# Column-layout attention: the softmax sums of two batches inverted on 112 partitions by way of small matmuls

## The chip, the cores and the metric

One core of one Trainium2 chip. The time is that of one execution on the device, in microseconds; it is the median of several runs. Beside these runs one execution was taken by the hardware profiler, and every row below is from that one.

## The reference

Attention over 4 batches, 12 heads, 448 positions and 64 dimensions, with a root-mean-square norm on q and k, then two feed-forward layers over the 1792 tokens:

```python
q_n, k_n = (rmsnorm(q, g_q), rmsnorm(k, g_k))
scores = scale * np.matmul(q_n, k_n.transpose(0, 1, 3, 2))
scores = scores - np.max(scores, axis=-1, keepdims=True)
attn = np.exp(scores)
attn = attn / (np.sum(attn, axis=-1, keepdims=True) + 1e-09)
attn_out = np.matmul(attn, v)
x = attn_out.transpose(0, 2, 1, 3).reshape(B * S, H * D)
g = x @ w_gate
x = (g * (1.0 / (1.0 + np.exp(-g))) * (x @ w_val)) @ w_out
h = x @ w_in
return (h * np.cos(h)) @ w_out2
```

## The kernel before

The work is done on pairs of heads: 4 batches by 6 pairs, 24 pairs in all. A pair's 896 query rows are 7 tiles of 128. The first two batches, pairs 0 to 11, are done in a first stage of their own, and they alone are touched by the change. Batches 2 and 3 have another way through attention, which runs beside the matmuls of the first feed-forward layer in the second stage. The second feed-forward layer follows.

In the first stage the scores are held transposed: keys on partitions, queries along the row. The stage is a list of steps (c_step, line 735), seven for each pair, which run from the first loads to step NCB + CXX + CXL. Each step calls, in this order: c_st (one tile of transposed scores, a matmul for q times k and one that takes off the row maximum, then the exponential on ScalarE, line 702), c_av (the exponentials times v in f32, line 712, in four parts a pair, at steps 1, 3, 5 and 6 after a shift of CAV), c_x, c_lo, c_s (scores ten steps ahead, only to find the maximum on VectorE, lines 669 and 670), c_row (the maxima turned into a row by a small matmul and copied to SBUF on ScalarE, lines 676 to 682, two steps ahead of the pair) and the preparation of later pairs: squares, the norm's power on GpSimd, scaling, the split into two f16 parts (h), and a DMA transpose into T. A scale (line 347) stands ahead of the power.

c_av writes two banks a pair, t and u, one for each head. The stationary operand has v in 64 of its columns and ones in the other 64, so that a bank holds the unnormalised output of the head in one half of its partitions and, in each of the 64 partitions of the other half, the same sum of exponentials. There is one bank t and one bank u, so the next pair's first c_av waits until both have been read. c_x (line 714) reads them with four ScalarE copies of 64 partitions by 448: the sums into r (lines 719 and 721, with 1e-9 added) and the outputs into ov (lines 720 and 722, scaled). It takes the reciprocal of all of r, 128 x 448, on VectorE (line 723), multiplies (line 726) and makes the high f16 part of x (line 727). Four steps later c_lo makes the low part on GpSimd (line 733). x is read by the second stage alone.

The order of the instructions is set by a planner, which takes them in the order in which they are written as their operands come free in its own timeline. In the first stage SyncE's DMAs and GpSimd's instructions are held in the order written (the InOrder helper, line 156); on TensorE the helper keep_in_program_order pins one instruction behind the one written just before it. PSUM has three banks "s" (c_s, c_row and small sums share them), three banks "c" for c_st, and t and u. After the first stage, banks c and u become part of the four banks "mm" of the second stage. The second stage begins with a score matmul of pair 12 (line 479, which needs its T), and then visits: 18 matmuls each, over three pairs' x (lines 1053 to 1055).

Of the kernel before, what the change touches and what calls it, by code (L numbers as in the profile page):

```python
# [9 lines left out]
F32 = mybir.dt.float32  # L10
# [4 lines left out]
AF = mybir.ActivationFunctionType  # L15
ALU = mybir.AluOpType
AX = mybir.AxisListType
PSUM = bass.MemoryType.PSUM
A0 = {'raw0': 2, 'h160': 1, 'sq0': 1, 'pr0': 6, 'T0': 2}
COL = {'B': 3, 'C': 3, 'w': 3, 'r': 2, 'o': 2, 'V': 2}  # L20
A1 = {'p16': 2, 'PT': 1, 'sq': 1, 'pr': 3, 'sm': 10, 'R': 1, 'rv': 1, 'raw': 1, 'h16': 1, 'T': 2}
CF = ('kl xl ql qm kf', 'rp vh nm xl qm sa 2', 'ql xl 0 2 5 6', 'ql xl 0 3 4 6')
LA = 5
# [7 lines left out]
CXX = 8  # L31
# [3 lines left out]
VMQ = 30  # L35
VMR = 8
VMO = 10
CXL = 4
VM2 = 46
CC1 = 22  # L40
CC2 = 29
# [123 lines left out]
def kernel(ctx: ExitStack, tc, q, k, v, g_q, g_k, w_gate, w_val, w_out, w2_in, w2_out, out):  # L165
    nc = tc.nc
# [3 lines left out]
    B, H, S, D = q.shape  # L170
    P = 128
    CO = 384
    NP = H // 2
# [9 lines left out]
    HP = P // 2  # L183
# [21 lines left out]
    ps_s = ctx.enter_context(tc.tile_pool(name="ps_s", bufs=3, space=PSUM))  # L205
# [7 lines left out]
    def xy_tile(more=False):  # L213
        return xy_pools[int(more)].tile([P, 2, S], F16, tag="xy", name="xy")

    def tmp():
        return tmp_p.tile([P, S], F32, tag="tmp", name="tmp")

    def bank(pool, tag):
        return pool.tile([P, 512], F32, tag=tag, name=tag)  # L220


    ident = const.tile([P, P], F32, name="ident")
# [12 lines left out]
    vs2 = const.tile([P, 2], F32, name="vs2")  # L236
# [38 lines left out]
    pools = {}  # L275
# [12 lines left out]
    NS = 2 * S // P  # L288
    NE = (NS + 1) // 2
    NB = NP * NS  # L290
    NCB = NC * NS
    prep = {}
# [96 lines left out]
    def x_inv(b):  # L389
        return vsc[:, 2 * b + 1:2 * b + 2]  # L390
# [225 lines left out]
    def ctile(nm, shape, dt, g=None):  # L616
        return c_p.tile(shape, dt, tag="c" + nm, name="c" + nm, bufs=COL[nm])

# [17 lines left out]
    def c_v(g):  # L636
        V = colv[g % 2]
        for h in range(2):
            hs = slice(HP * h, HP * h + HP)
            src = v[g // NP, 2 * (g % NP) + h].rearrange("(q t) d -> q t d", t=NS)  # L640
            sync.dma_start(V[:HP, :4 - h, h, hs], src[:, 0:NS - h:2])
            sync.dma_start(V[HP:, :3, h, hs], src[:, 1:NS:2])
            if h:
                sync.dma_start(V[HP:, 3, h, hs], src[:, NS - 1])

    def c_T(g):
        pg = prep[g]
        T = pg["T"] = pool("T", g).tile([P, 2 * NS, P], F16, tag="T", name="T")
        sync.dma_start_transpose(T, pg["h16"].rearrange("p g d -> p (g d)"))

    def c_copy(g):
        pg = prep[g]
        T = pg["T"]
        Bq = pg["B"] = ctile("B", [P, NS, P], F16)
        C = colc[g % 3][0]
        nc.vector.tensor_copy(Bq[:HP], T[HP:, :NS])
        nc.vector.tensor_copy(T[HP:, :NS], T[:HP, :NS])
        nc.scalar.activation(C[:HP], T[:HP, NS:], AF.Copy)

    def c_s(n):  # L660
        g, t = divmod(n, NS)
        pg = prep[g]
        if t == 0:
            pg["m"] = pools["sm"].tile([P, 3, 8], F32, tag="sm", name="sm")
        ps = bank(ps_s, "s")
        T = pg["T"]
        for h in range(2):
            hs = slice(HP * h, HP * h + HP)
            nc.tensor.matmul(ps[hs, :S].rearrange("p (t q) -> p t q", q=HP), T[:, t, hs], T[:, NS:, h::2], start=True, stop=True)
        nc.vector.tensor_reduce(pg["m"][:, 0, t:t + 1], ps[:, :S], axis=AX.X, op=ALU.max)  # L670

    def c_row(g):
        pg = prep[g]
        W = colc[g % 3][1]
        m = pg["m"][:, 0, :NS]
        nc.vector.tensor_scalar(W[:, :, 0], m, 2.0 ** -14, None, op0=ALU.mult)
        nc.vector.scalar_tensor_tensor(W[:, :, 32], m, 2.0 ** -14, W[:, :, 0], op0=ALU.mult, op1=ALU.subtract)
        for t0, t1 in ((0, 4), (4, NS)):
            ps = bank(ps_s, "s")
            for t in range(t0, t1):  # L680
                nc.tensor.matmul(ps[HP:, (t - t0) * P:(t - t0 + 1) * P], W[:, t], id16, start=True, stop=True)
            nc.scalar.activation(
                pg["B"][HP:, t0:t1], ps[HP:, :(t1 - t0) * P].rearrange("p (t q) -> p t q", q=P), AF.Copy,
            )

    def c_st(n):
        g, i = divmod(n, NS)
        pg = prep[g]
        T, Bq, C = pg["T"], pg["B"], colc[g % 3][0]
        ps = bank(ps_c, "c")  # L690
        h0, j = CT[i]
        e = col[g, i] = pool("pr", g, n).tile([P, S], F32, tag="pr", name="pr")
        for k, (wt, off, mv) in enumerate(((T, NS, T), (C, 0, Bq))):
            for h in ((0, 1) if h0 is None else (h0,)):
                hs = slice(HP * h, HP * h + HP)
                rows = hs if h0 is None else slice(0, P)
                k0 = (off + 2 * j) * P + h
                w = wt.rearrange("p t q -> p (t q)")[:, k0:min(k0 + 2 * P - 1, (off + NS) * P):2]
                nc.tensor.matmul(
                    ps[rows, :S].rearrange("p (t q) -> p t q", q=HP), w, mv[:, :NS, hs], start=(k == 0), stop=(k == 1),  # L700
                )
        nc.scalar.activation(e, ps[:, :S], AF.Exp, scale=esc)

    def c_av(g, j):
        pg = prep[g]
        if j == 0:
            pg["o"] = (bank(ps_t, "t"), bank(ps_u, "u"))
        for h in range(2):
            hs = slice(HP * h, HP * h + HP)
            rows = slice(0, P) if j < 3 else hs  # L710
            e = col[g, 2 * j + h] if j < 3 else col[g, NS - 1]
            nc.tensor.matmul(pg["o"][h][:, :S], colv[g % 2][rows, j, h], e[rows], start=(j == 0), stop=(j == 3))

    def c_x(g):
        pg = prep.pop(g)
        o = pg["o"]
        r, ov = ctile("r", [P, S], F32), ctile("o", [P, S], F32)
        vb = vs2[:, g // NP:g // NP + 1]
        nc.scalar.activation(r[:HP], o[0][HP:, :S], AF.Copy, bias=1e-9)
        nc.scalar.activation(ov[:HP], o[0][:HP, :S], AF.Copy, scale=vb[:HP])  # L720
        nc.scalar.activation(r[HP:], o[1][:HP, :S], AF.Copy, bias=1e-9)
        nc.scalar.activation(ov[HP:], o[1][HP:, :S], AF.Copy, scale=vb[HP:])
        nc.vector.reciprocal(r, r)
        x = X[g] = xy_tile()
        xs = tmp()
        nc.vector.tensor_tensor(xs, ov, r, op=ALU.mult)
        nc.scalar.activation(x[:, 0], xs, AF.Copy)
        xlo[g] = xs

# [2 lines left out]
    def c_lo(g):  # L732
        gps.tensor_sub(X[g][:, 1], xlo.pop(g), X[g][:, 0])

    def c_step(n):
        if 0 <= n < NCB:
            c_st(n)
        m = n - CAV
        if m >= 0 and m % NS in (1, 3, 5, 6) and m < NCB:
            c_av(m // NS, (1, 3, 5, 6).index(m % NS))  # L740
        m = n - CXX
        if m >= 0 and m % NS == 0 and m < NCB:
            c_x(m // NS)
        m = n - CXX - CXL
        if m >= 0 and m % NS == 0 and m < NCB:
            c_lo(m // NS)
        m = n + CSM
        if 0 <= m < NCB:
            c_s(m)
        m = n + CRW  # L750
        if m >= 0 and m % NS == 0 and m < NCB:
            c_row(m // NS)
        if n < NCB:
            s_prep(n)

    PREP = (
        ("load", p_load), ("vload", p_vload), ("sqk", lambda g: p_sq(g, 1)), ("sqq", lambda g: p_sq(g, 0)),
# [6 lines left out]
    def ph(g):  # L764
        return 2 if g < NC else 2 + g // NP
# [3 lines left out]
    def s_prep(n):  # L769
        for nm, f in PREP:  # L770
            for g in range(NPAIR):
                if NS * g + OFF[ph(g)][nm] - (CSH if g < NC else 0) == n:
                    if g < NC and nm in ("vhi", "vlo"):
                        continue
                    if g < NC and nm == "vload":
                        c_v(g)
                    elif g < NC and nm == "T":
                        c_T(g)
                    elif g < NC and nm == "sw":
                        c_copy(g)  # L780
                    else:
                        f(g)
# [466 lines left out]

    for n in range(1 - LEAD, NCB + CXX + CXL + 1):  # L1250
        for f, at in ((v_max, 0), (v_row, VMR), (v_out, VMO)):
# [38 lines left out]
    for bn, per in blocks:  # L1290
# [15 lines left out]
        for qn in range(per):  # L1306
# [3 lines left out]
            kind, c = pc["kind"], pc["c"]  # L1310
# [47 lines left out]
    for c in range(NH):  # L1358
        j0 = j
        j += 2  # L1360
        for b in range(B):
            ps = [bank(ps_s, "s"), bank(ps_t, "t")] if nh % 3 == 2 else [bank(ps_m, "mm") for _ in range(2)]
# [28 lines left out]
    while j < len(pieces):  # L1391
        ps = [None] * nt
# [49 lines left out]
```

## Time and profile before

| | |
|---|---|
| median of 3 runs | 1311.82 us (1310.14 to 1314.35) |
| the profiled execution | 1312.33 us |
| its span, first to last instruction | 1310.6 us |
| TensorE busy, share of the span | 1201.9 us, 92% |
| VectorE (DVE) busy | 858.2 us, 65% |
| ScalarE (ACT) busy | 661.3 us, 50% |
| GpSimd (POOL) busy | 404.4 us, 31% |
| mean granted TensorE clock | 0.974 of full speed |

The shares are averages over stages with different limits. In the rows further down, PE is TensorE's matmuls and PEld its weight loads, L719 is line 719 of the kernel, and an arrow stands for "waits for" or "made from". An f32 matmul shows as two instructions, one for each of its passes.

### The profile page before, as it was taken

How to read it: one execution, taken by the hardware profiler on the slowest of the kernel's cores; microseconds unless marked ns; L12 is line 12 of the kernel's file. 1: busy time of each engine (PE TensorE's matmuls, PEld its weight loads, DVE VectorE, ACT ScalarE, POOL GpSimd, SP SyncE). 2: the span in 40 equal slices, each digit the busy share in tenths (PEclk: the TensorE clock that was granted, in tenths of full speed). 3: DMA queues.
4: the chain of work that ended last, by engine and by line, in shares of the span. 5: the costliest groups of instructions: out<-in, count | busy, mean ns of one | idle time of the engine just before them, and what ended most of it. 6: DMA issues, size and time to landing. Idle time of an engine off the chain costs nothing. (4 is left out here: it accounts for less than half of the span.)

```text
span 1310.6 us, 18041 instructions
## 1 busy us (share of the span) xinstructions
PE 1201.9 (92%) x6460; PEld 677.1 (52%) x6460; DVE 858.2 (65%) x1555; ACT 661.3 (50%) x1246; POOL 404.4 (31%) x309
## 2 busy tenths in 40 slices
PE   1888797989889998999999999999999998999998
PEld 0333233444665446844468555855555545666665
DVE  5888966989978897067854498477788886100000
ACT  3677565656456543265653455457777775100000
POOL 7645302433622345035453013504332322000000
PEclk9799898999989999999999999999999999999999
DMA  5534734678797879579668697640112237522121
GB/s 139 138 73 82 191 99 118 179 187 228 225 247 221 204 208 287 183 175 225 150 133 257 235 315 263 235 157 1 50 49 73 73 133 261 177 72 94 61 91 43
DMA packets 218425, 207.34 MB, mean 158 GB/s; under 512 B 143584, under 2 KB 173792, under 8 KB 218336
## 3 DMA queue, kind: packets, MB, share of 16 engines
q1 hardware_dynamic: 218336, 206.20, 55.5%
q8 instruction: 50, 0.82, 0.2%
q14 instruction: 39, 0.32, 0.1%
HBM read 134.35 MB, written 41.53 MB: 134 GB/s over the span
## 5 line engine op out<-in xcount | busy, mean ns | idle before, releaser
L1053 PE MATMUL mm<-xy,wp 128*128 128x448 f16 x840 | 297.5, 355 | 2.7 <-DVE ga L1092 2.6
L1054 PE MATMUL mm<-xy,wp 128*128 128x448 f16 x840 | 297.2, 354 | 0.0
L1055 PE MATMUL mm<-xy,wp 128*128 128x448 f16 x840 | 295.6, 354 | 0.0
L1066 PEld LDWEIGHTS <-g 128*128 128x128 f16 x1344 | 131.5, 98 | 91.0 <-issue 4.1
L1053 PEld LDWEIGHTS <-wp 128*128 128x128 f16 x960 | 95.8, 100 | 99.8 <-issue 19.2
L1055 PEld LDWEIGHTS <-wp 128*128 128x128 f16 x960 | 94.5, 98 | 87.4 <-issue 2.0
L1054 PEld LDWEIGHTS <-wp 128*128 128x128 f16 x960 | 94.7, 99 | 84.5 <-issue 5.7
L156 POOL TENSOR_TENSOR g<-tmp,g 128x448 f16<-128x448 f32 x64 | 71.0, 1122 | 175.7 <-ACT g L1212 175.7
L1053 PE MATMUL mm<-g,wp 128*128 128x448 f32 x288 | 108.3, 376 | 3.8 <-ACT mm L1113 2.6
L1054 PE MATMUL mm<-g,wp 128*128 128x448 f32 x288 | 106.8, 371 | 1.7 <-POOL g L156 1.7
L1055 PE MATMUL mm<-g,wp 128*128 128x448 f32 x288 | 106.3, 370 | 0.0
L156 POOL TENSOR_TENSOR g<-ga,g 128x448 fp32r<-128x448 f32 x48 | 68.3, 1436 | 112.2 <-ACT g L1102 111.8
L1066 PE MATMUL mm<-wp,g 128*128 128x384 f16 x576 | 99.2, 326 | 3.7 <-DVE tmp L1208 3.7
L1066 PE MATMUL s<-wp,g 128*128 128x384 f16 x576 | 99.3, 326 | 0.0
L156 POOL TENSOR_TENSOR wp<-w,wp 128x768 fp32r<-128x768 f32 x36 | 70.3, 1958 | 74.4 <-ACT wp L993 42.8
L498 ACT ACTIVATE pr<-s,sm,esc 128x448 f32<-128x448 f32 x84 | 60.2, 717 | 62.2 <-DVE sm L492 55.5
L488 DVE TENSOR_REDUCE sm<-s 128x1 f32<-128x448 f32 x84 | 51.0, 615 | 44.1 <-PE s L479 44.1
L1224 ACT ACTIVATE tmp<-mm,osc 128x384 f32<-128x384 f32 x8 | 4.6, 580 | 148.6 <-PE mm L1066 147.8
L156 POOL TENSOR_TENSOR ri<-ss,half 128x14 f32<-128x14 f32 x24 | 63.3, 2639 | 41.6 <-DVE ss L347 32.8
L893 DVE SCALAR_TENSOR_TENSOR w<-raw,w 128x768 int32<-128x768 int32 x68 | 75.1, 1107 | 0.5
L894 DVE SCALAR_TENSOR_TENSOR w<-raw,w 128x768 int32<-128x768 int32 x68 | 75.0, 1104 | 0.5
L156 POOL TENSOR_TENSOR p<-pr,p 128x448 f16<-128x448 f32 x36 | 42.4, 1181 | 100.4 <-ACT p L522 65.0
(174 smaller groups left out, 2263.2 us busy)
## 6 DMA issues: line engine op xcount, KB each, us to landing
raw<-in_moe_w_out_dram SPq DMA_DIRECT2D x28, 768.0 KB, 5.8
raw<-in_moe_w_in_dram SPq DMA_DIRECT2D x16, 768.0 KB, 5.8
raw<-in_moe_w_gate_dram SPq DMA_DIRECT2D x12, 768.0 KB, 5.8
raw<-in_moe_w_val_dram SPq DMA_DIRECT2D x12, 768.0 KB, 5.6
wp<-scr_gate SPq DMA_DIRECT2D x24, 384.0 KB, 4.5
w<-scr_out SPq DMA_DIRECT2D x24, 384.0 KB, 4.2
wp<-scr_val SPq DMA_DIRECT2D x24, 384.0 KB, 5.0
wp<-scr_out SPq DMA_DIRECT2D x24, 384.0 KB, 3.0
```

Of the source, the lines that this page charges most:

```text
L156: r = f(*args, **kw)
L488: nc.vector.tensor_reduce(sm[:, 0, t:t + 1], slot[n][:, :S], axis=AX.X, op=ALU.max)
L498: nc.scalar.activation(e, slot.pop(n)[:, :S], AF.Exp, bias=sm[:, 1, t:t + 1], scale=esc, accum_out=sm[:, 2, t:t + 1],)
L893: nc.vector.scalar_tensor_tensor(wi, hi, -0x40000000, wi, op0=ALU.bitwise_and, op1=ALU.bitwise_or)
L894: nc.vector.scalar_tensor_tensor(wi, lo, 29, wi, op0=ALU.logical_shift_right, op1=ALU.bitwise_or)
L1053: nc.tensor.matmul(ps[f][:, :S], wh[:, s], x[:, 0], start=(first and i == 0), stop=False)
L1054: nc.tensor.matmul(ps[f][:, :S], wh[:, s], x[:, 1], start=False, stop=False)
L1055: nc.tensor.matmul(ps[f][:, :S], wl[:, s], x[:, 0], start=False, stop=(last and i == n - 1))
L1066: nc.tensor.matmul(ps[:, :CO], x[:, a, p0:p0 + P], rhs, start=st, stop=sp)
L1224: nc.scalar.activation(osb, ps[:, :CO], AF.Copy, scale=ci)
```

## The change

c_x now copies the two banks whole, 128 partitions by 448, on ScalarE, and is done. One step later c_inv moves the sums: for each of four pieces of 112 queries and each head, a matmul with the copied bank as the stationary operand and one column of the identity as the moving one puts the 112 sums of that piece on 112 partitions. The eight results are eight columns of one s bank. VectorE adds 1e-9 and scales them (one instruction) and takes the reciprocal, 112 x 8. One step on, c_back brings them back: eight matmuls with such a column, repeated 64 times, as the stationary operand and the identity as the moving one, into the halves of another s bank. One step on, c_mul multiplies on VectorE, half by half and straight from the bank, and makes the high part of x. c_lo comes eight steps after c_x in place of four. The tiles r are gone, the tiles o are four in place of two.

```diff
--- before.py
+++ after.py
@@ -17,7 +17,7 @@
 AX = mybir.AxisListType
 PSUM = bass.MemoryType.PSUM
 A0 = {'raw0': 2, 'h160': 1, 'sq0': 1, 'pr0': 6, 'T0': 2}
-COL = {'B': 3, 'C': 3, 'w': 3, 'r': 2, 'o': 2, 'V': 2}
+COL = {'B': 3, 'C': 3, 'w': 3, 'o': 4, 'V': 2}
 A1 = {'p16': 2, 'PT': 1, 'sq': 1, 'pr': 3, 'sm': 10, 'R': 1, 'rv': 1, 'raw': 1, 'h16': 1, 'T': 2}
 CF = ('kl xl ql qm kf', 'rp vh nm xl qm sa 2', 'ql xl 0 2 5 6', 'ql xl 0 3 4 6')
 LA = 5
@@ -35,7 +35,11 @@
 VMQ = 30
 VMR = 8
 VMO = 10
-CXL = 4
+CXL = 8
+CXI = 1
+CXB = 2
+CXM = 3
+QC = 112
 VM2 = 46
 CC1 = 22
 CC2 = 29
@@ -712,18 +716,43 @@
             nc.tensor.matmul(pg["o"][h][:, :S], colv[g % 2][rows, j, h], e[rows], start=(j == 0), stop=(j == 3))
 
     def c_x(g):
+        pg = prep[g]
+        o = pg["o"]
+        ov = pg["ov"] = [ctile("o", [P, S], F32) for _ in range(2)]
+        for h in range(2):
+            nc.scalar.activation(ov[h], o[h][:, :S], AF.Copy)
+
+    def c_inv(g):
+        pg = prep[g]
+        ps = bank(ps_s, "s")
+        for c in range(4):
+            for h in range(2):
+                one = HP - HP * h
+                tc.keep_in_program_order(nc.tensor.matmul(
+                    ps[:QC, 2 * c + h:2 * c + h + 1], pg["ov"][h][:, QC * c:QC * c + QC], ident[:, one:one + 1], start=True, stop=True,
+                ))
+        r = pg["r"] = pools["sm"].tile([P, 3, 8], F32, tag="sm", name="sm")
+        nc.vector.tensor_scalar(r[:QC, 0], ps[:QC, :8], 1e-9, x_inv(g // NP)[:QC], op0=ALU.add, op1=ALU.mult)
+        nc.vector.reciprocal(r[:QC, 1], r[:QC, 0])
+
+    def c_back(g):
+        pg = prep[g]
+        ps = pg["rb"] = bank(ps_s, "s")
+        r = pg["r"]
+        for c in range(4):
+            for h in range(2):
+                tc.keep_in_program_order(nc.tensor.matmul(
+                    ps[HP * h:HP * h + HP, QC * c:QC * c + QC], r[:QC, 1, 2 * c + h:2 * c + h + 1].to_broadcast([QC, HP]),
+                    ident[:QC, :QC], start=True, stop=True,
+                ))
+
+    def c_mul(g):
         pg = prep.pop(g)
-        o = pg["o"]
-        r, ov = ctile("r", [P, S], F32), ctile("o", [P, S], F32)
-        vb = vs2[:, g // NP:g // NP + 1]
-        nc.scalar.activation(r[:HP], o[0][HP:, :S], AF.Copy, bias=1e-9)
-        nc.scalar.activation(ov[:HP], o[0][:HP, :S], AF.Copy, scale=vb[:HP])
-        nc.scalar.activation(r[HP:], o[1][:HP, :S], AF.Copy, bias=1e-9)
-        nc.scalar.activation(ov[HP:], o[1][HP:, :S], AF.Copy, scale=vb[HP:])
-        nc.vector.reciprocal(r, r)
         x = X[g] = xy_tile()
         xs = tmp()
-        nc.vector.tensor_tensor(xs, ov, r, op=ALU.mult)
+        for h in range(2):
+            hs = slice(HP * h, HP * h + HP)
+            nc.vector.tensor_tensor(xs[hs], pg["ov"][h][hs], pg["rb"][hs, :S], op=ALU.mult)
         nc.scalar.activation(x[:, 0], xs, AF.Copy)
         xlo[g] = xs
 
@@ -738,12 +767,10 @@
         m = n - CAV
         if m >= 0 and m % NS in (1, 3, 5, 6) and m < NCB:
             c_av(m // NS, (1, 3, 5, 6).index(m % NS))
-        m = n - CXX
-        if m >= 0 and m % NS == 0 and m < NCB:
-            c_x(m // NS)
-        m = n - CXX - CXL
-        if m >= 0 and m % NS == 0 and m < NCB:
-            c_lo(m // NS)
+        for f, d in CEND:
+            m = n - CXX - d
+            if m >= 0 and m % NS == 0 and m < NCB:
+                f(m // NS)
         m = n + CSM
         if 0 <= m < NCB:
             c_s(m)
@@ -752,6 +779,8 @@
             c_row(m // NS)
         if n < NCB:
             s_prep(n)
+
+    CEND = ((c_x, 0), (c_inv, CXI), (c_back, CXB), (c_mul, CXM), (c_lo, CXL))
 
     PREP = (
         ("load", p_load), ("vload", p_vload), ("sqk", lambda g: p_sq(g, 1)), ("sqq", lambda g: p_sq(g, 0)),
```

## Rows read from the trace of the kernel before

**Rows 1.** busy time by stretch: length, PE, PEld, DVE, ACT, POOL, clock, DMA

```profile
155.97:178.38 22.41, 16.36 (x71) 6.40 (x71) 14.24 (x28) 11.16 (x19) 2.79 (x3) 0.85 0.27 67
178.38:190.78 12.40, 11.20 (x56) 4.97 (x55) 9.77 (x20) 10.23 (x18) 1.04 (x1) 1.00 0.37 110
...
52.57:215.90 163.33, 136.61 (x575) 54.16 (x574) 137.17 (x216) 115.59 (x207) 57.86 (x43) 0.92 0.45 112
```

**Rows 2.** waits of TensorE's matmuls, 52.57 to 215.90: total, times, longest

```profile
PE s L681 <- DVE cw L677: 8.4, 3, 5.9
PE s L669 <- DVE sm L670: 4.0, 5, 1.1
PE s L669 <- ACT cB L682: 3.4, 3, 1.6
PE t L712 <- ACT pr L702: 3.2, 4, 1.2
PE c L699 <- ACT cB L682: 2.9, 2, 1.7
PE s L681 <- DVE vm L365: 2.9, 1, 2.9
PE s L681 <- DVE ss L347: 1.5, 1, 1.5
```

**Rows 3.** groups by line, 52.57 to 215.90: busy us, mean ns | idle before

```profile
L723 DVE RECIPROCAL cr<-cr 128x448 f32<-128x448 f32 x11 | 32.4, 2947 | 1.1 <-ACT cr L721 0.8
...
L720 ACT ACTIVATE co<-t,vs 64x448 f32<-64x448 f32 x11 | 6.9, 628 | 0.1
L726 DVE TENSOR_TENSOR tmp<-co,cr 128x448 f32<-128x448 f32 x11 | 6.8, 616 | 0.4 <-ACT pr L702 0.4
L719 ACT ACTIVATE cr<-t 64x448 f32<-64x448 f32 x12 | 6.5, 540 | 9.5 <-PE u L712 9.3
```

**Rows 4.** busy time by stretch, the stretch just behind, columns as in rows 1

```profile
222.00:262.00 40.00, 40.00 (x214) 19.41 (x212) 34.36 (x67) 20.99 (x41) 16.97 (x11) 0.95 0.55 146
```

**Rows 5.** single lines: count, ns min/median/max (L904: busy us, mean ns)

```profile
L1208 DVE SCALAR_TENSOR_TENSOR tmp<-tmp,mm x44: 606/621/623, 882.1 to 1098.0; 128x448 f32<-128x448 f32 x44
...
L904 DVE RECIPROCAL wsc<-winv 128x1 f32<-128x1 f32 x1 | 0.2, 164 | 0.0
...
L1113 ACT ACTIVATE mm<-mm x36: 533/541/547, 343.7 to 861.2; 128x448 f32<-128x448 f32 x36
```

**Rows 6.** timeline of TensorE from 178.68: start, length, instruction, count

```profile
178.68 0.50 PE L919 MATMUL s<-nm,full 128*128 128x1 f32 x4
...
179.04 0.54 PE L699 MATMUL c<-cB,cC 128*128 128x448 f16 x2
...
179.51 0.79 PE L669 MATMUL s<-T 128*64 128x448 f16 x6
```

**Rows 7.** timeline of TensorE, the last c_av of the third pair

```profile
95.28 0.64 PE L712 MATMUL t<-pr,cV 64*128 64x448 f32 x1
...
95.29 0.64 PE L712 MATMUL u<-pr,cV 64*128 64x448 f32 x1
...
95.76 0.54 PE L712 MATMUL t<-pr,cV 64*128 64x448 f32 x1
```

**Rows 8.** timeline, the longest wait of the row matmuls

```profile
159.14 2.93 DVE L723 RECIPROCAL cr<-cr 128x448 f32<-128x448 f32 x1
...
162.76 0.63 PE L681 MATMUL s<-id,cw 128*64 128x128 f16 x4 [5.90 <-DVE cw L677]
```

**Rows 9.** timeline, what leads to the second stage's first matmul

```profile
204.62 2.95 DVE L723 RECIPROCAL cr<-cr 128x448 f32<-128x448 f32 x1
...
207.49 0.11 DVE L347 TENSOR_SCALAR ss<-ss 128x14 f32<-128x14 f32 x1
...
220.96 0.58 PE L479 MATMUL s<-T 128*64 128x448 f16 x2 [5.09 <-DMA T<-h]
```

**Rows 10.** waits, 40 to 216, GpSimd's longest: us in total, times, longest

```profile
POOL xy L156 <- ACT xy L727: 90.3, 9, 20.9
```

## The prediction

> **What bounds the kernel now.** I read the busy times by stretch first, to see which engine leads while the changed lines run; then who made TensorE wait there; then the groups of the changed lines; then the stretch behind. The stretch is from the first L719 (52.57 us) to the twelfth (215.90): eleven intervals in 163.33 us, 14.85 each. In it DVE is busy 137.17 us, TensorE 136.61, ACT 115.59 [rows 1]. So two engines lead almost level; TensorE idles 26.7 us (163.33 - 136.61). The granted clock is 0.92 on average: 1.00 where an interval is short (12.4 us from 178.38) and 0.85 in the longest one (22.4 us from 155.97). The clock has two levels, 1.2 and 2.4 GHz, so part of each long interval ran at the lower one.
>
> The waits name the 26.7 us: 16.8 are put down to DVE (8.4 + 4.0 + 2.9 + 1.5), 9.5 to ACT (3.4 + 3.2 + 2.9) [rows 2]. The reader is to see that nobody waits for the reciprocal as such: x is not read before the next stage. It costs by standing in DVE's queue ahead of the maxima and of the row that feeds the next pair. What it costs there: 2947 ns a time, and its four ACT copies twice 540 + 628, 2.34 us (two for each of a pair's banks) [rows 3].
>
> Behind the stretch TensorE is busy 40.00 us of 40.00 [rows 4]. So I let time won or lost before it come out whole at the end, and price whatever TensorE work spills into it in full.
>
> **The change part by part.** The sums are per pair of heads; there are twelve pairs.
>
> DVE: out go the reciprocal, 2.95, and one product, 0.616 [rows 3]. In come two products of 64 rows that read PSUM; the nearest row, a product with a PSUM operand, takes 0.62, and I take that for each, since time goes with the 448 columns. In come also a scale and a reciprocal of eight columns; a reciprocal of one column takes 0.164 and I take 0.2 for each [rows 5]. That is 3.56 out, 1.64 in: 1.9 us less per pair, 23 us over twelve, none of it yet on the path.
>
> ACT: four copies of 64 rows become two of 128. A plain copy of 128 x 448 from PSUM takes 0.541 [rows 5], so 2.34 becomes 1.08: 1.26 less per pair.
>
> TensorE, first set (c_inv): eight f32 matmuls with one moving column each, and each f32 matmul stands in the trace as two passes. The nearest row has four passes of that shape, with weights of 128 columns; they start at 178.68 and the next matmul starts at 179.04, so 0.09 us a pass [rows 6]. Sixteen are 1.44 us. Below that they could be 112/128 of it, 1.26.
>
> TensorE, second set (c_back): eight f32 matmuls of 112 columns, into the upper and the lower 64 rows of a bank in turn. The nearest f32 row with two halves is the last c_av: its t and u passes run at the same time, and the second passes start 0.48 us after the first, for 448 columns [rows 7]. At 112 columns that is 0.12; in pairs 8 x 0.12 = 0.96 us, one after another 16 x 0.12 = 1.92. I take 0.96, because in the f16 row of exactly this column shape six matmuls (three pairs of 448 columns) need 0.79 us with their loads [rows 6]. Together 2.4 us a pair, between 2.2 and 3.4; twelve make 28.8. I let all of it count: c_inv is pinned behind the first c_av of the next pair and c_back behind a c_st, that is inside the run of matmuls in which TensorE itself is the bound and not in its waits.
>
> What comes off the path. (a) The four copies begin when a pair's last c_av ends, and the copy of the next pair's rows and its exponentials stand behind them on ACT. TensorE waited for ACT nine times for 9.5 us [rows 2], about 1.06 a time, against 1.26 saved: I take 8.5. (b) Of DVE's 16.8, the longest wait, 5.9 us to 162.76, has the whole reciprocal in it (159.14 to 162.07) [rows 8]: 2.9 go. Of the other 10.9 I take 6: the 2.9 behind a v maximum stay, since the change touches nothing of it, and 2 of the rest, where the maxima wait for matmuls themselves. Together 9. What is late next there is the chain of maxima itself. (c) The clock: 8% of 163.33 is 13.1 us. With 17.5 of 26.3 us of waits gone I take half, 6.5. (d) The next stage's first matmul starts at 220.96, 5.09 us late, on a transpose. That goes back to a scale at 207.49 which came out of DVE's queue right behind the reciprocal of 204.62 [rows 9]. 2.9 us go; then TensorE's own last c_av is what is late. (e) c_lo moves from four to eight steps behind c_x. On POOL, kept in program order, it waited 90.3 us for x [rows 10], and the subtractions that feed the next transposes stood behind it. Its operand now comes three steps later and it five after that, one step more of room than before; I take 1 us. No DMA is added and SP's order holds the same issues. Off together: 8.5 + 9 + 6.5 + 2.9 + 1 = 27.9.
>
> What I cost at nothing: the banks. Each set takes one of the three "s" banks, c_back's until both products are done. The cover is that DVE no longer stands for 2.95 us with three maxima behind it. Without that cover c_s waits as it does now, 4.0 us in all [rows 2]. The last pair's chain has no loss either: its x is first needed after three visits of 18 matmuls.
>
> The sum: 28.8 - 27.9 = +0.9. The profiled execution took 1312.33 us (span 1310.6, 1.7 around it); 1313.2. The median of the runs, 1311.82, is 0.5 lower, so 1312.7, given as **1313**. The pattern is an exchange: DVE is freed, and TensorE takes its place as the bound.
>
> **The rivals.** *The new matmuls fall into waits.* If the planner puts them where TensorE would still idle, the 8.8 us that I left (26.3 - 17.5) take that much of the 28.8; and with shorter gaps the clock stays up, 6.6 us more. 1312.7 - 8.8 - 6.6 = 1297. For it: TensorE at 1.00 in the interval that starts at 178.38 [rows 1], where few waits fell. Against it: the pins.
>
> *The halves don't pair (the other side).* In c_back each weight load and each pass goes alone, 1.92 instead of 0.96: 3.4 us a pair, 40.3 in all, +12.4 and 1324. The point from which it decides is 27.9 / 12 = 2.3 us of TensorE per pair; over 2.65 the whole is slower by more than a measurement can tell. For it: the 0.48 us of the f32 halves is more than twice what a pair of f16 matmuls takes in the six, 0.2. Against it: those halves do start together [rows 6, 7].
>
> The Trainium skill speaks for this rival. Its page "TensorE: Matmul & The Clock Gate", Part 3 ("The mechanism"), says that a weight load overlaps a running matmul only where its row group is another one; all of c_back's loads use the same rows, so by that rule none would be hidden. The trace doesn't hold to it for f16: the six matmuls above cover all rows and have a load each; three times 448 columns take 0.56 us at 2.4 GHz, so 0.23 is left of 0.79 for six loads and the way through the array [rows 6]. For f32 weights of half the columns no row here shows it, and this is why the rival keeps a real chance.
>
> *The copies were not the wait.* If the row copy comes late through TensorE itself, (a) and half of (b) fall away: 1312.7 + 13 = 1326. The waits speak against it, since both name ACT and DVE as last; it is in the slow cases' upper end.
>
> **How the numbers follow.** About 0.3% (3.9 us) is what a measurement of this kernel can tell from no change. The exchange has 0.42 (1305 to 1320: 0.12 faster, 0.19 same, 0.11 slower), the matmuls in the waits 0.32 (0.29 faster, 0.03 same), the halves that don't pair 0.18 and the copies that were not the wait 0.08 (0.01 same, 0.25 slower between them). Sums: faster 0.41, same 0.23, slower 0.36. The low end is the first rival with half of what c_inv may come in under its price (1 us of 2), 1296; the high end takes the last two rivals and a few us on top of 1324 for c_s waiting on banks, 1328. The likeliest case's own range is 1305 to 1320.
>
> **What would show it.** Right: in the same twelve-pair stretch DVE's busy time falls by about 21 us and TensorE's rises above DVE's by 15 or more; c_inv's sixteen passes take near 1.44 us and c_back's 0.96, with upper and lower halves starting together; TensorE's waits for DVE and ACT sum to under 12 us; the clock of the stretch is over 0.92; the last c_x starts within some 4 us of 215.90. The second stage's first matmul comes 1 to 3 us after the last c_av, not 5. Wrong: c_back's passes evenly spaced at 0.12 or more; or the waits still at 20 us; or DVE's waits now for c_back (a new term that I left out); or, on the other side, intervals all near 12 us, which would mean that the passes cost TensorE nothing.

## The result, and the profile after

| | median us | ratio to the kernel before, 95% interval |
|---|---|---|
| the kernel before, beside it | 1312.97 | |
| the changed kernel | 1321.82 (1320.42 to 1324.71, 4 runs) | 1.0085 [1.0061, 1.0109] |

The change costs 0.85%. The ratio is taken between the executions of the same chip and goes with an interval, so all comparisons below are made by ratios; times 1311.8 us it is 11.2 us (8.0 to 14.3). The profiled execution of the changed kernel took 1324.71 us, its span 1322.8. Lines of the new functions: c_x L723, c_inv L731 (matmuls), L735 and L736 (scale, reciprocal), c_back L744, c_mul L755, the high part of x L756. Lines carried over from the kernel before have numbers four higher: c_s is L673 and L674, c_row L680 to L686, c_st L703, c_av L716, and GpSimd's helper is L160.

First the busy times by stretch, the same stretch as in [rows 1], from the first c_x to the twelfth, and what follows it (columns as there).

```profile
52.44:229.40 176.96, 155.91 (x927) 79.52 (x926) 124.44 (x246) 103.40 (x187) 60.28 (x44) 0.98 0.48 114
229.40:235.32 5.92, 2.99 (x17) 2.91 (x17) 2.67 (x4) 2.69 (x6) 1.58 (x2) 0.72 0.72 141
240.00:280.00 40.00, 40.00 (x240) 20.31 (x238) 35.45 (x68) 22.48 (x46) 16.88 (x12) 1.00 0.54 148
```

The stretch is 13.6 us longer (176.96 against 163.33). TensorE is busy 19.3 us more and DVE 12.7 less, so TensorE now leads by 31. The clock went from 0.92 to 0.98. Yet TensorE is still idle for 21.05 us (176.96 - 155.91), against 26.7. The engine became the bound, and four fifths of its idle time stayed. Behind the stretch it is again busy throughout, as in [rows 4].

Next, for whom TensorE's matmuls wait there (in total, times, longest), to be held against [rows 2].

```profile
PE s L685 <- DVE cw L681: 11.1, 7, 4.5
PE s L744 <- DVE sm L736: 1.9, 1, 1.9
PE c L703 <- ACT cB L686: 1.8, 2, 1.6
PE s L673 <- ACT cB L686: 1.4, 6, 0.3
PE s L673 <- DVE tmp L755: 1.4, 1, 1.4
PE s L673 <- DVE sm L674: 1.3, 2, 1.0
PE t L716 <- ACT pr L706: 0.7, 2, 0.3
```

Waits for ACT fell from 9.5 to 3.9 us (1.8 + 1.4 + 0.7). Waits for DVE did not fall: with two more of 0.4 and 0.3 they are 16.4, against 16.8, although the 2.95 us reciprocal is gone. Together the two kinds are still 20.3 us. The waits for DVE now come seven times in eleven pairs from cw, the scaled maxima, in place of three times.

The groups of the changed lines (busy us, mean ns | idle before):

```profile
L731 PE MATMUL s<-ident,co 128*112 128x1 f32 x176 | 18.1, 233 | 0.0
L755 DVE TENSOR_TENSOR tmp<-co,s 64x448 f32<-64x448 f32 x20 | 12.4, 619 | 5.5 <-PE s L744 5.3
L744 PE MATMUL s<-ident,sm 112*64 112x112 f32 x176 | 10.6, 263 | 1.9 <-DVE sm L736 1.9
...
L681 DVE SCALAR_TENSOR_TENSOR cw<-sm,cw 128x7 f16<-128x7 f32 x10 | 6.5, 652 | 0.2
L680 DVE TENSOR_SCALAR cw<-sm 128x7 f16<-128x7 f32 x10 | 5.2, 516 | 0.2
L735 DVE TENSOR_SCALAR sm<-s,vsc 112x8 f32<-112x8 f32 x11 | 2.4, 220 | 2.6 <-PE s L731 2.6
L736 DVE RECIPROCAL sm<-sm 112x8 f32<-112x8 f32 x11 | 2.2, 196 | 0.1
```

Every single duration is near its price: copies 540 ns, products 619, scale and reciprocal 220 and 196. Two things are to be seen beside that. DVE stands idle for 5.3 us before the products, waiting for c_back. And the two little instructions that make cw take 516 and 652 ns. In the kernel before:

```profile
L677 DVE SCALAR_TENSOR_TENSOR cw<-sm,cw 128x7 f16<-128x7 f32 x10 | 4.9, 494 | 0.2
...
L676 DVE TENSOR_SCALAR cw<-sm 128x7 f16<-128x7 f32 x10 | 2.2, 218 | 0.1
```

The timeline of one interval shows how the wait comes about.

```profile
89.21 1.64 PE L731 MATMUL s<-ident,co 128*112 128x1 f32 x16
...
90.78 0.39 PE L673 MATMUL s<-T 128*64 128x448 f16 x2
...
95.10 0.99 PE L744 MATMUL s<-ident,sm 112*64 112x112 f32 x16
...
95.92 0.57 PE L673 MATMUL s<-T 128*64 128x448 f16 x4
96.14 1.25 DVE L755 TENSOR_TENSOR tmp<-co,s 64x448 f32<-64x448 f32 x2 [1.25 <-PE s L744]
...
97.42 1.16 DVE L674 TENSOR_REDUCE sm<-s 128x1 f32<-128x448 f32 x2
...
98.08 1.03 POOL L160 TENSOR_TENSOR xy<-tmp,xy 128x448 f16<-128x448 f32 x1 [7.15 <-ACT xy L756]
...
98.61 0.54 DVE L680 TENSOR_SCALAR cw<-sm 128x7 f16<-128x7 f32 x1
...
99.07 1.03 POOL L160 TENSOR_TENSOR h<-rqk,h 128x448 f16<-128x448 f32 x1
99.18 0.96 DVE L681 SCALAR_TENSOR_TENSOR cw<-sm,cw 128x7 f16<-128x7 f32 x1
...
100.20 0.58 PE L685 MATMUL s<-id,cw 128*64 128x128 f16 x7 [1.01 <-DVE cw L681]
```

c_inv needs 1.57 us until the next matmul starts, c_back 0.82. But DVE stands for 1.25 us until c_back is done, then works 1.25 us on the products, and only then come the last two maxima, cw, and the row that the next pair's scores need. The products themselves are in no hurry: x is read in the next stage.

The products do more than stand in the queue. As soon as the high part of x is made from them, GpSimd subtracts it (98.08), and in its order the split h follows (99.07). Both run beside cw, and each of cw's two instructions ends within 0.05 us of one of GpSimd's. At the 0.19 us each that they take elsewhere they would have been done 1.1 us sooner; TensorE waited 1.01 us. Four of the seven waits for cw are of this kind, 1.01 us each. The longest, 4.5 us, is another: there cw is not slow, but two instructions on the next stage's weights (w, 1.27 and 0.94 us) stand before it and between its two parts in VectorE's queue.

At the end of the stage (before: 5.57 us from the last c_x at 215.90 to the first matmul of a visit at 221.47):

```profile
229.98 0.36 PE L731 MATMUL s<-ident,co 128*112 128x1 f32 x2 [1.09 <-ACT co L723]
230.35 1.24 DVE L755 TENSOR_TENSOR tmp<-co,s 64x448 f32<-64x448 f32 x2
...
231.62 0.58 ACT L756 ACTIVATE xy<-tmp 128x448 f16<-128x448 f32 x1 [1.69 <-DVE tmp L755]
232.11 0.53 ACT L723 ACTIVATE co<-u 128x448 f32<-128x448 f32 x1
...
232.68 2.77 PE L731 MATMUL s<-ident,co 128*112 128x1 f32 x14 [2.35 <-ACT co L723]
```

It is 5.92 us now, from 229.40 to the first matmul of a visit at 235.32. The wait for the transpose is gone from there; in its place the last pair's c_inv waits twice, 3.44 us, for the copies of banks t and u. The second copy stands on ACT behind the high part of the pair before, which waits for that pair's products.

### The profile page after: what moved, and what is told of

Its sections match the earlier page's. It is cut to its first block, busy times and chain, and to the rows that moved or that the text cites. A ratio compares the mean times of both kernels' runs of the same rounds, so it can differ in the third digit from the quotient of the medians.

```text
span 1322.8 us, 18802 instructions
## 1 busy us (share of the span) xinstructions
PE 1223.4 (92%) x6844; PEld 704.8 (53%) x6844; DVE 837.1 (63%) x1579; ACT 645.7 (49%) x1222; POOL 409.2 (31%) x309
## 5 line engine op out<-in xcount | busy, mean ns | idle before, releaser
L160 POOL TENSOR_TENSOR g<-tmp,g 128x448 f16<-128x448 f32 x64 | 71.2, 1126 | 175.4 <-ACT g L1241 175.4
L160 POOL TENSOR_TENSOR g<-ga,g 128x448 fp32r<-128x448 f32 x48 | 64.4, 1353 | 121.6 <-ACT g L1131 121.4
L160 POOL TENSOR_TENSOR wp<-w,wp 128x768 fp32r<-128x768 f32 x36 | 73.6, 2050 | 78.0 <-ACT wp L1022 47.0
L160 POOL TENSOR_TENSOR p<-pr,p 128x448 f16<-128x448 f32 x36 | 44.0, 1226 | 124.0 <-ACT p L526 97.4
L922 DVE SCALAR_TENSOR_TENSOR w<-raw,w 128x768 int32<-128x768 int32 x68 | 77.5, 1145 | 0.5
L921 DVE TENSOR_SCALAR w<-raw 128x768 int32<-128x768 int32 x68 | 50.2, 744 | 37.8 <-DMA w<-scr_out 9.8
L160 POOL TENSOR_TENSOR ri<-ss,half 128x14 f32<-128x14 f32 x24 | 64.6, 2690 | 29.3 <-DVE ss L351 28.6
```

The lines of the kernel that those rows point to most:

```text
L160: r = f(*args, **kw)
L921: nc.vector.tensor_scalar(wi, hi, 3, 0x3FFFFFF8, op0=ALU.logical_shift_left, op1=ALU.bitwise_and)
L922: nc.vector.scalar_tensor_tensor(wi, hi, -0x40000000, wi, op0=ALU.bitwise_and, op1=ALU.bitwise_or)
```

## The experiments

Twelve runs, in three groups. The first takes the change's savings without its cost, the second takes parts of the cost away, the third looks for a way to have the savings without it. The runs of the first group leave out the division or give a head the wrong sums, and those with half of c_inv leave out the second head's sums: they serve for their time alone.

| run | median us | ratio, 95% interval |
|---|---|---|
| whole copies alone | 1299.09 | 0.9901 [0.9871, 0.9931] |
| no reciprocal alone | 1303.34 | 0.9924 [0.9895, 0.9954] |
| both, nothing added | 1285.53 | 0.9797 [0.9770, 0.9823] |
| changed kernel, products late | 1314.46 | 1.0025 [1.0006, 1.0045] |
| changed kernel, half of c_inv | 1314.95 | 1.0031 [1.0014, 1.0047] |
| both of these | 1308.84 | 0.9991 [0.9973, 1.0008] |
| changed kernel, no pins | 1319.12 | 1.0056 [1.0037, 1.0074] |
| aligned banks | 1343.92 | 1.0248 [1.0227, 1.0269] |
| aligned banks, transposes | 1327.03 | 1.0122 [1.0101, 1.0142] |
| the same, halves in a row | 1290.00 | 0.9843 [0.9817, 0.9869] |
| whole copies, transposes | 1294.69 | 0.9886 [0.9862, 0.9911] |
| the same, products on GpSimd | 1299.92 | 0.9926 [0.9904, 0.9947] |

### What the savings are worth

```diff
-        nc.scalar.activation(r[:HP], o[0][HP:, :S], AF.Copy, bias=1e-9)
-        nc.scalar.activation(ov[:HP], o[0][:HP, :S], AF.Copy, scale=vb[:HP])
-        nc.scalar.activation(r[HP:], o[1][:HP, :S], AF.Copy, bias=1e-9)
-        nc.scalar.activation(ov[HP:], o[1][HP:, :S], AF.Copy, scale=vb[HP:])
+        nc.scalar.activation(ov, o[0][:, :S], AF.Copy)
+        nc.scalar.activation(r, o[1][:, :S], AF.Copy, bias=1e3)
...
-        nc.vector.tensor_tensor(xs, ov, r, op=ALU.mult)
+        nc.vector.scalar_tensor_tensor(xs, ov, 2.0 ** -16, r, op0=ALU.mult, op1=ALU.mult)
```

> The kernel before with the banks copied whole and nothing else: two ScalarE copies of 128 x 448 a pair in place of four of 64 x 448; the full reciprocal and the product stay (the operands are the two banks as they lie, so this leaves out that each head's output meets its own sums). If the four copies stood on the path, as term (a) had it, this alone is 7 to 10 us faster than before, and TensorE's waits for ACT in the stretch fall from 9.5 to under 4. If what ends those waits is TensorE's own order, it is within 3 us of before.

The first run has the copies alone, without the last two lines shown. The second run keeps the four copies, drops the line `nc.vector.reciprocal(r, r)` and has the product of the last two lines; the third does both, with 1e-9 in place of 1e3.

> The kernel before with the reciprocal left out (the product multiplies by the sums and a constant), four copies as before; the division is what is left out. If the reciprocal in DVE's queue cost what terms (b), (d) and half of (c) had (9 + 2.9 + 3), this is 13 to 17 us faster than before and TensorE's waits for DVE fall from 16.8 to about 8. If those waits come from the chain of maxima itself and not from the reciprocal, it is 3 to 7 us faster and the waits stay over 12.

> Both at once: whole copies and no reciprocal, no new matmuls (the division is left out, and each head's own sums). This is all that the change takes away, without what it adds. The prediction's sum has 27.9 us for it, so about 1285. Then the added matmuls and products cost the rest up to the kernel after, some 37. If DVE's share was overrated, it is 12 to 20 us faster than before, and what the change adds costs 21 to 29.

The copies alone bring 0.99%, 13 us, more than the 7 to 10 expected, though TensorE's waits for ACT in the stretch fell to 5.6 us (2.5 + 1.9 + 0.7 + 0.5) and not under 4; the reciprocal alone 0.76%, 10 us, less than the 13 to 17. Together they bring 2.03%, 26.6 us (23.2 to 30.2), about the sum. The stretch of the third run, and what held TensorE in the first:

```profile
50.97:196.24 145.27, 133.23 (x575) 51.50 (x574) 103.99 (x205) 100.50 (x186) 60.80 (x43) 0.98 0.50 129
```

```profile
PE s L681 <- DVE cw L677: 15.3, 6, 5.2
```

With shorter copies alone, cw is still the longest wait. With the reciprocal gone alone, the waits for DVE fell from 16.8 to 5.4 us (some 8 expected), but those for ACT rose from 9.5 to 11.2. With both, TensorE idles 12.0 us (145.27 - 133.23). Against this run the changed kernel's stretch is 31.7 us longer: 22.7 us of it TensorE's busy time (155.91 - 133.23), 9.0 idle time. The whole costs of the change are 1.0085 - 0.9797, 2.9% or 37.8 us; what of it lies outside the stretch, some 6 us, was not taken apart.

### What the cost is made of

```diff
-CXB = 2
-CXM = 3
+CXB = 4
+CXM = 5
```

> The kernel after with c_back two steps later (4) and c_mul two steps later (5), so that the two products are written behind the row of the next pair and not ahead of it. If the products in DVE's queue ahead of the last maxima hold up that row (they wait for c_back and take 1.25 us a pair), the row comes 1 to 2 us a pair earlier and the time falls by 8 to 16 us from the kernel after, to 1306 to 1314. If TensorE's passes alone set the pair's length, the time stays within 3 us of the kernel after.

```profile
50.02:222.86 172.84, 156.99 (x927) 80.04 (x926) 114.14 (x248) 103.79 (x188) 61.79 (x44) 0.99 0.49 116
```

```profile
PE s L673 <- DVE sm L674: 4.1, 5, 1.8
PE t L716 <- ACT pr L706: 3.2, 4, 2.2
PE s L673 <- ACT cB L686: 2.3, 4, 0.7
```

```profile
L680 DVE TENSOR_SCALAR cw<-sm 128x7 f16<-128x7 f32 x10 | 2.0, 196 | 0.1
```

These are its stretch, the longest waits there, and the first of cw's instructions. The wait for cw is not among the waits any more; for DVE 5.9 us are left in all, against 16.4. That edit changes nothing but when c_back and the products are issued, so 0.6%, 7.9 us of the 37.8 (some 4 to 12 by the two intervals, just short of the 8 to 16 expected), is their place in the queues. Three things moved with that place and are not parted by this run: the products no longer stand ahead of the maxima; cw no longer runs beside GpSimd (over the 0.19 us each, its instructions take 0.3 us more in all, against 8.0 in the changed kernel); and c_back stands elsewhere on TensorE. Nor did all of the wait become time: the waits for ACT rose from 3.9 to 7.9 us, and TensorE's idle time fell by 5.2 us, to 15.85 (172.84 - 156.99).

```diff
-            for h in range(2):
-                one = HP - HP * h
-                tc.keep_in_program_order(nc.tensor.matmul(
-                    ps[:QC, 2 * c + h:2 * c + h + 1], pg["ov"][h][:, QC * c:QC * c + QC], ident[:, one:one + 1], start=True, stop=True,
-                ))
+            tc.keep_in_program_order(nc.tensor.matmul(
+                ps[:QC, 2 * c:2 * c + 2], pg["ov"][0][:, QC * c:QC * c + QC], ident[:, HP:HP + 2], start=True, stop=True,
+            ))
```

> The changed kernel with four small matmuls in place of eight in c_inv: the bank of the first head alone is the stationary operand and two columns of the identity move, so the second head's own sums are left out and the first head's are used for both. Eight passes fewer per pair at about 0.10 us each, 0.8 us. Theory (the passes stand on TensorE's path and count in full, 28.8 of the 36.3 us that the change adds): 12 x 0.8 = 9 us less, about 1312 to 1314. Rival (the passes lie in time in which TensorE would wait anyway, and the added time is banks, pins and DVE's queue): within 3 us of the changed kernel, 1319 to 1323.

Its timeline, c_inv and the next matmul:

```profile
85.44 0.86 PE L729 MATMUL s<-ident,co 128*112 128x2 f32 x8
86.23 0.39 PE L673 MATMUL s<-T 128*64 128x448 f16 x2
...
221.83 0.95 PE L729 MATMUL s<-ident,co 128*112 128x2 f32 x8 [0.63 <-ACT co L723]
```

Eight passes need 0.79 us where sixteen needed 1.57; a second moving column costs nothing. Twelve times 0.78 are 9.4 us; 0.54%, 7.1 us (some 3 to 11), came out at the end, which cannot be told from 9.4. But the edit also takes a wait away: c_inv now needs the copy of bank t alone, and at the end of the stage it waits 0.63 us in place of 3.44. Some 3 of the 7 us may be that wait, so the run does not show by itself what the passes cost.

> The changed kernel with both single edits together: products three steps after c_inv's in place of one behind c_back (c_back at step 4, c_mul at step 5), and c_inv in eight passes in place of sixteen, the second head's own sums left out. Theory (queue place and passes are separate costs): the late products bring it to 1314, eight passes at 0.10 us take 5 to 9 us more off, 1305 to 1310, below the kernel before. Rival (both edits remove the same wait): no better than the better of the two, 1313 to 1316.

Both edits together bring 0.94%, 12.3 us, of the 15.0 that they bring singly. They are two costs and not one; whether they overlap cannot be told, with intervals of some 4 us on each of these figures. The kernel, with the second head's sums left out, is level with the one before. What is left to the 26.6 us of the savings, some 25 us, is the other half of c_inv, c_back, and what was not taken apart: the two banks, and DVE's work on two products of 64 rows in place of one of 128.

In the fourth of these runs `keep_in_program_order` is left out in c_inv and c_back.

> The changed kernel with c_inv's and c_back's matmuls not pinned behind the instruction written before them; the planner places them. Theory (the passes cost what they take wherever they stand, and c_mul's place in DVE's queue is the new wait): within 4 us of the changed kernel, 1318 to 1326. Rival (the pins hold TensorE for copies that come late, most of all for the last pair, where 3.4 us of waits stood before c_inv): 3 to 8 us less, 1314 to 1319.

```profile
231.90 1.97 PE L731 MATMUL s<-ident,co 128*112 128x1 f32 x16 [0.66 <-ACT co L723]
233.73 0.35 PE L1082 MATMUL mm<-xy,wp 128*128 128x448 f16 x1
```

The last c_x is at 231.32 here, so the next stage starts 2.4 us behind it and not 5.92: the pins did make the end of the stage. But its stretch grew to 179.90 us, and in total 0.3% is gained, which the two intervals do not quite tell from nothing. Neither of the two expectations can be dropped by that.

### The savings without the cost

The aim of c_inv and c_back is a short reciprocal. Two other ways to it were tried. One writes both heads' outputs into one bank and both heads' sums into the other, so that two whole copies give aligned tiles:

```diff
+        for i in range(2):
+            for h in range(2):
+                hs = slice(HP * h, HP * h + HP)
+                ws = hs if i == 0 else slice(HP - HP * h, P - HP * h)
...
+                nc.tensor.matmul(pg["o"][i][hs, :S], colv[g % 2][rows, j, h, ws], e[rows], start=(j == 0), stop=(j == 3))
```

> The kernel before with the outputs of both heads in one bank and the sums of both in the other: each of c_av's matmuls of 128 weight columns becomes two of 64, and the upper and lower halves of a bank are written side by side. Two copies of 128 rows in place of four of 64, the whole reciprocal kept, no matmul of the change. If halves pair as c_back's did (16 passes in 0.82 us), TensorE's time stays and the gain is that of the two whole copies measured without them, 13.8 us: 1296 to 1303. If the halves of f32 matmuls of 448 columns don't pair, c_av's passes double: 84 pass pairs of 0.46 us or more, over 30 us slower.

The other shrinks the reciprocal with VectorE's own transposes, here on top of the aligned banks:

```diff
-        nc.vector.reciprocal(r, r)
+        nc.vector.transpose(rt, r)
+        nc.vector.reciprocal(ri[:, :14], rt.rearrange("p (n k) -> p n k", k=32)[:, :, 0])
+        nc.vector.transpose(r, ri[:, :14].unsqueeze(2).to_broadcast([P, 14, 32]))
```

> The same, and the reciprocal shrunk on VectorE itself: the sums are transposed in blocks of 32 by 32, one reciprocal of 14 columns is taken, and a second transpose of the repeated column brings them back. No matmul is added. If a transpose of 448 columns takes about what a product does (0.6 us), DVE is at 0.6 + 0.2 + 0.6 in place of 2.95 a pair, 1.5 us less, and half of what leaving out the reciprocal brought on top of whole copies (13.6 us) should come: about 1290 to 1296. If a transpose takes 1.3 us or more, nothing is gained on the kernel with aligned banks alone.

Both were slower than before, by 2.5% and 1.2%. Between the two, the transposes took 1.26%, 16.5 us, off. The timeline and the stretch of the second show why both lost:

```profile
109.79 0.91 PE L714 MATMUL t<-pr,cV 128*64 128x448 f32 x2
110.54 0.91 PE L714 MATMUL u<-pr,cV 128*64 128x448 f32 x2
111.39 0.36 PE L699 MATMUL c<-T 128*128 128x448 f16 x1
```

```profile
53.49:235.47 181.98, 176.79 (x755) 58.53 (x753) 115.81 (x238) 105.20 (x188) 59.21 (x43) 1.00 0.43 108
```

The planner issued, for one head, its half of t and then its half of u. Both are the same half of the columns, nothing of the other side stands beside them, and each pair of passes takes 0.75 us as if it had all 128 columns: TensorE is busy 176.79 us of 181.98. The third run changes the order and pins it:

```diff
-        for i in range(2):
-            for h in range(2):
+        for n, (i, h) in enumerate(((0, 1), (0, 0), (1, 1), (1, 0))):
...
+                if n:
+                    tc.keep_in_program_order(mm)
```

> The kernel with aligned banks and the transposed reciprocal, with c_av's four half matmuls of a step held in one row on TensorE: upper and lower half of the outputs, then upper and lower half of the sums. Where the earlier one lost, the trace showed two halves of the same side one after another, 0.75 us a matmul of two passes, and only here and there an upper beside a lower one, 0.38 a pass pair. Theory (it lost by halves that stood alone): in a row three of the four changes of side overlap, five slots of 0.375 us in place of eight, so 1.1 us a pair over the kernel before for each three steps: 1290 + 13 = 1303, between 1299 and 1311. Rival (halves of this length do not overlap when each waits for its weights): no better than the 1327 measured, within 5 us.

```profile
95.36 0.97 PE L713 MATMUL t<-pr,cV 128*64 128x448 f32 x4
96.16 0.92 PE L713 MATMUL u<-pr,cV 128*64 128x448 f32 x4
97.01 0.36 PE L699 MATMUL c<-T 128*128 128x448 f16 x1
```

```profile
50.95:196.90 145.95, 137.34 (x753) 46.82 (x751) 115.50 (x237) 103.18 (x184) 57.82 (x43) 0.99 0.50 126
```

```profile
L728 DVE STREAM_TRANSPOSE cr<-ci 128x448 f32<-128x448 f32 x11 | 7.1, 641 | 0.2
L726 DVE STREAM_TRANSPOSE cr<-cr 128x448 f32<-128x448 f32 x11 | 7.0, 634 | 0.0
```

Four passes of two heads now take 0.80 and 0.85 us, about what two passes of one head took. With the same instructions in another order the time falls from 1327.03 to 1290.00; even the theory's 1303 was too high. The stretch is 145.95 us, 0.7 more than with the whole saving and nothing added. A transpose takes 0.64 us, so division costs DVE 2.1 us a pair (641 + 634 + a reciprocal of 229 + a product of 616), and TensorE is as busy as before (137.34 against 136.61). Of the versions that compute the whole result this is the fastest, ahead of the two kernels by 1.6% and 2.4%.

The other order of ideas leaves the banks as they were, takes the changed kernel's two whole copies, and transposes on VectorE (two of 64 rows there, one of 128 back):

```diff
+        for h in range(2):
+            nc.scalar.activation(ov[h], o[h][:, :S], AF.Copy)
+        for h in range(2):
+            hs, ss = slice(HP * h, HP * h + HP), slice(HP - HP * h, P - HP * h)
+            nc.vector.transpose(rt[hs], ov[h][ss])
```

> The kernel before, its banks as they were, with the two whole copies of the changed kernel, and the reciprocal shrunk on VectorE by 32 by 32 transposes (two of 64 rows, a scale and a reciprocal of 14 columns, one transpose of 128 rows back, two products of 64 rows). TensorE gets nothing to do. VectorE: 3 x 0.64 + 0.4 + 2 x 0.62 = 3.6 us a pair, as before (3.56), but in pieces of 0.64 or less; ScalarE 1.26 less. Theory (the copies are worth 13.8 us alone, and the new matmuls are what eats the gain): 1294 to 1302, faster than both kernels. Rival (VectorE's total is what bounds once the copies are short): no gain over 1306.

```profile
51.01:205.61 154.60, 136.89 (x575) 53.53 (x574) 134.45 (x272) 101.91 (x186) 58.25 (x43) 0.94 0.48 124
```

1.1% faster than before, 1294.69: the theory. DVE is busy nearly as long as before (134.45 us of a stretch of 154.60, against 137.17), while the longest piece of the division is 0.66 us in place of 2.95. What that brings is not shown by the times: whole copies alone had 0.99%, and the two intervals overlap. In the traces TensorE's waits for cw fall from 15.3 us with whole copies alone to 2.3.

> The same, with the two products on GpSimd in place of VectorE. VectorE has 1.24 us a pair less, 2.3 in all. Theory (VectorE's share that is left is worth about what leaving out 2.95 us was worth on top of the copies, 13.6 us, by length): 5 us less than the run with the products on VectorE, 1289 to 1297. Rival (GpSimd, held in program order, stands for products of about 1.1 us each while the split for the next transposes waits behind them, or its work slows VectorE's small instructions): equal or slower, 1297 to 1310.

In this one `nc.vector.tensor_tensor` of the two products becomes `gps.tensor_tensor`. It lost 0.4% on the run before it, just more than the two intervals leave to noise. Its waits, TensorE's longest and GpSimd's longest:

```profile
PE s L669 <- DVE sm L670: 12.0, 7, 5.1
...
POOL tmp L156 <- DVE cr L728: 25.2, 6, 8.8
```

The rival's range, 1297 to 1310, holds. GpSimd, in program order, stands up to 8.8 us for the transpose. That the power for a later pair's norm, VectorE's scaling and the maxima are late behind it follows from the order of the program; no run tried it by itself.

## Why the prediction was right or wrong

The forecast was 1313, an even exchange, with a range of 1296 to 1328; 1321.82 lies in the range, just outside the likeliest case's own (1305 to 1320). That it lies in the range is in part luck: the upper end was made of two rivals, halves that do not pair and copies that were not the wait, and neither is what happened. The pattern held: DVE freed, TensorE its heir. The sign did not: slower by over 0.3% had 0.36, less than the 0.41 for faster. Of the prediction's own signs of being wrong two came: the waits stayed at 20.3 us (16.4 + 3.9), and VectorE waited for c_back (5.3 us). The last c_x started at 229.40, not near 215.90.

**The gains as a sum were right.** 27.9 predicted, 26.6 (23.2 to 30.2) measured with nothing added. Its parts were not, as the terms below show.

**The price of the matmuls was right.** c_inv 1.57 us (1.44 predicted), c_back 0.82 (0.96): 2.39 a pair against 2.4. TensorE's busy time in the stretch rose by 22.7 us over the run with the whole saving, 2.1 a pair. Whether all of it counts at the end is open: half of c_inv should have given 9.4 us and gave 7.1, with a wait for a copy taken away beside it.

**The halves do pair.** c_back's sixteen passes at 0.82 us are eight times 0.10. The rival that had them one after another, at 1.92 us, falls, though its time of 1324 was close: the time was lost elsewhere. By the rule of the Trainium skill's page "TensorE: Matmul & The Clock Gate", Part 3 ("The mechanism"), a weight load is hidden only by a matmul on another row group; here all loads use the same rows, and opposite halves of the columns ran at full pairs in c_back and in the aligned kernel, so these runs do not hold to it.

**The step that failed is term (b) together with what I cost at nothing.** I let 9 of DVE's 16.8 us of waits go; 0.4 went. They do go when nothing is added: the run with both savings has TensorE idle for 12.0 us, not 21. c_back and c_mul put them back, by their place. I counted the wait of c_back's bank and its cover, but not what comes behind the products on VectorE: two instructions that nobody needs soon, which first stand for c_back and then delay the last two maxima and cw, and which set off GpSimd's subtraction just where cw runs beside it. Issued two steps later they give back 7.9 us (some 4 to 12). How much of that is the queue and how much the slow cw is not shown. Measured is +11.2 where the working had +0.9, 10.3 apart: 7.9 of it is this; the other 2.4 (1.3 of gains, 27.9 against 26.6, and 1.1 of the rest of the additions, 37.8 - 7.9 = 29.9 against 28.8) is less than these runs can tell from nothing. The prediction's last part named the wait for c_back as a term that it had left out; it should have been in the sum.

**(a) Copies.** ACT's waits fell by 5.6 us, not 8.5; alone, whole copies bring more than (a) had, 13 us. Only part of that is seen in the first stage, where the first visit starts 6.6 us earlier (214.88 against 221.47); where the rest comes from is open. **(c) The clock** rose from 0.92 to 0.98 although little of the idle time went; counted as in the prediction, 6% of the new stretch are 10.6 us, where I had taken 6.5. **(d)** was wrong by its cause: with both savings and nothing added TensorE still waits 4.13 us for that transpose. In the changed kernel it is in time because the last c_av ends 13 us later (it was issued at 215.83, before at 215.53), and the last pair's pinned c_inv waits in its place. "The last pair's chain has no loss" was wrong: x was not late, but the pin let TensorE wait for copies on the way to it. **(e)** GpSimd's wait for x fell only from 90.3 to 77.4 us up to the last c_x; its 1 us can't be seen.

**DVE**'s busy time fell by 12.7 us in the stretch, not 21. The changed lines did as priced (39.2 us out [rows 3], 17.0 in, 12.4 + 2.4 + 2.2). Against it stand 4.6 us that cw took longer and ten more instructions of other kinds that fell into the longer stretch (30 more in all, of which the changed lines are 42 - 22).

Not settled: how the 7.9 us divide between the queue and the slow cw, how much c_back costs alone, whether its bank costs anything, and whether the pins do.

## What to carry to other kernels

When work is moved to another engine and its result brought back, the return is a wait in the queue of the engine that uses it: ask what stands behind that user, and issue it late if the result is not urgent. A long instruction that hurts only by what is queued behind it can be shortened where it is: two transposes of 0.64 us and a reciprocal of 0.23 in VectorE's own queue did the work of 2.95 us and beat a shorter one that needs 2.4 us of the engine that bounds. And the length of a small instruction ahead of the engine that bounds is to be read together with what runs beside it.

## What the runs showed of the hardware beyond that

- f32 matmuls of 64 weight columns ran two at a time where one of the other half followed directly: a matmul alone, or behind one of the same half, takes 0.75 us for its two passes; two of opposite halves take 0.80 us for their four. The order is worth 37 us here (1327.03 to 1290.00).
- A transposition of 32 by 32 blocks takes VectorE 0.64 us for 448 columns of 64 or 128 rows, with a repeated column as its source too; the reciprocal of as many columns takes 2.95.
- VectorE's two instructions on 7 columns (cw) ran 336 times in the 14 traces. Wherever GpSimd did nothing beside them, or only the power on 14 columns, they took 0.12 to 0.20 us (219 times). All 90 that took longer, up to 1.04 us, ran beside one of GpSimd's instructions on 448 columns, and 89 of them ended within 0.05 us of its end. That GpSimd holds them up fits this; no run took GpSimd's instruction away by itself.
